# Pacing the weight loads of the last attention head, and five smaller reorderings, in a fused forward and backward pass

## The chip, the cores and the metric

The kernel runs on one core of one Trainium2 chip. The metric is device microseconds (us) of one execution on that core. A kernel is run several times, and its median is quoted.

## The reference

One attention block (32 heads of width 128 over 2048 positions, model width 576, cached K and V) times the silu of a gated feed-forward block (hidden width 4608), both on the layer norm of `x`, with a residual. The kernel returns the forward result and the gradients of eight arguments.

```python
def _fwd_reference(A_x, A_k_cache, A_v_cache, A_wq, A_wo, B_x, B_w_gate, B_w_up, B_w_down):
    ...
    x = A_x
    xn = _layernorm(x, axis=-1)
    s = _A_ref(xn, A_k_cache, A_v_cache, A_wq, A_wo)      # softmax attention, then @ wo
    g = _silu(_B_ref(xn, B_w_gate, B_w_up, B_w_down))     # (sigmoid(xn@wg) * (xn@wu)) @ wd
    return x + s * g

def reference(A_x, ..., grad_out):
    ...
    _out, _vjp = jax.vjp(_f, A_x, A_k_cache, A_v_cache, A_wq, A_wo, B_w_gate, B_w_up, B_w_down)
    return (_out, *_vjp(grad_out))
```

## The kernel before

The kernel begins with the layer norm and the feed-forward block's forward pass. Attention, forward and backward, one head after the other, is the long stage in the middle. Then comes the first late stage (the product with `wo`), the feed-forward's backward pass, the gradient of `wq`, and a last stage for the gradient of `x`.

**Attention.** A head has two phases of 16 slots each, one slot for 128 query rows. Phase 1 makes a slab of probabilities with `exp` on ScalarE, and SyncE transposes it by DMA. Phase 2 makes the backward slab from `dp` in two halves, and that slab is transposed by DMA too. What uses a transposed slab (`tail1`, `tail2`) comes five slots later (the skew).

```python
def transpose_slab(hs, qt, name):
    T = wpt.tile([P, NT, P], bf, name=name, tag="PT")
    nc.sync.dma_start_transpose(T[:], hs.slabs[qt][:])          # PT or dST, 512 KB
    return T
...
def main2(hs, qt, hf):                                          # phase 2, half hf of row block qt
    Pq, hsl = hs.slabs[qt], slice(hf * HW_, (hf + 1) * HW_)
    dp = ps_big.tile([P, HW_], f32, name="dp", tag="big")
    ... # 2 matmuls into dp
    if hf == NHF - 1:
        nc.vector.scalar_tensor_tensor(Pq[:, hsl], dp[:], hs.negdelta[:, qt:qt + 1], Pq[:, hsl], op0=ALU.add, op1=ALU.mult)
        hs.dST[qt] = transpose_slab(hs, qt, "dST")
    else:
        t = wt.tile([P, HW_], bf, name="t")
        nc.scalar.activation(t[:], dp[:], AF.Identity, bias=hs.negdelta[:, qt:qt + 1], scale=1.0)
        nc.vector.tensor_tensor(Pq[:, hsl], t[:], Pq[:, hsl], op=ALU.mult)
```

**Loads for the first late stage.** The stage after attention needs all of `wo` (4608 KB) and the attention outputs ("on rows") transposed. Both go into buffers that fall free during the last head. `wo` is loaded by GpSimd, four heads at a time.

```python
bl = 2 * NT * (H - 1) + NT                                      # slot where phase 2 of the last head begins
for view, h0, n, dead in wo_parts:
    for k in range(0, n, 4):
        at = (1 + k // 4, q(skew + 1), q(skew + 2), q(skew + 4), q(skew + 5))[dead]
        put(bl + q(at), 0, lambda view=view, h0=h0, k=k, n=n: load_wo_rows(view, h0, k, min(k + 4, n)))
for st in range(min(2, NT)):
    put(bl + NT + skew * st, 0, lambda st=st: load_oT(oTs[st], st))
```

**The layer norm** is interleaved with feed-forward matmuls. A `turn` is five TensorE transposes of a normed row block.

```python
def turn_step():
    if todo["turn"] and not (todo["norm"] and todo["norm"][0] <= todo["turn"][0]):
        st = todo["turn"].pop(0)
        turn(st)
```

**Further on**, `load_heads` loads the on rows and the `dq` rows of the first head group together. In the last stage ScalarE's and VectorE's row sums go into two halves of one small tile, `cc`.

Of the kernel before, what the change touches and what calls it, by code (L numbers as in the profile page):

```python
# [66 lines left out]
def kernel(  # L67
# [164 lines left out]
    with tc.tile_pool(name="pa", bufs=1) as pa:  # L232
# [75 lines left out]
        with tc.tile_pool(name="a1w", bufs=1) as wp:  # L308
# [37 lines left out]
            with tc.tile_pool(name="a0", bufs=3) as sb0, tc.tile_pool(name="a0ps", bufs=2, space=PSUM) as ps0, \  # L346
# [70 lines left out]
                def turn_step():  # L417
                    if todo["turn"] and not (todo["norm"] and todo["norm"][0] <= todo["turn"][0]):
                        st = todo["turn"].pop(0)
                        turn(st)  # L420
                        return st
# [168 lines left out]
    def attention(fast):  # L590
        with ExitStack() as es:
# [15 lines left out]
            acc_box[0] = acc_alloc  # L607

# [85 lines left out]
            def main2(hs, qt, hf):  # L694
                Pq, hsl = hs.slabs[qt], slice(hf * HW_, (hf + 1) * HW_)
                dp = ps_big.tile([P, HW_], f32, name="dp", tag="big")
                for c in range(HW_ // CH):
                    nc.tensor.matmul(dp[:, c * CH:(c + 1) * CH], lhsT=hs.dOT[:, qt * P:(qt + 1) * P],  # L698
                                     rhs=hs.VT[:, hf * HW_ + c * CH: hf * HW_ + (c + 1) * CH], start=True, stop=True)
                if hf == NHF - 1:  # L700
                    nc.vector.scalar_tensor_tensor(Pq[:, hsl], dp[:], hs.negdelta[:, qt:qt + 1], Pq[:, hsl], op0=ALU.add, op1=ALU.mult)  # L701
                    hs.dST[qt] = transpose_slab(hs, qt, "dST")
                else:
                    t = wt.tile([P, HW_], bf, name="t")
                    nc.scalar.activation(t[:], dp[:], AF.Identity, bias=hs.negdelta[:, qt:qt + 1], scale=1.0)  # L705
                    nc.vector.tensor_tensor(Pq[:, hsl], t[:], Pq[:, hsl], op=ALU.mult)  # L706

# [68 lines left out]
            def q(k):  # L776
                return min(k, NT - 1)
# [46 lines left out]
            for view, h0, n, dead in wo_parts:  # L824
                for k in range(0, n, 4):
                    at = (1 + k // 4, q(skew + 1), q(skew + 2), q(skew + 4), q(skew + 5))[dead]
                    put(bl + q(at), 0, lambda view=view, h0=h0, k=k, n=n: load_wo_rows(view, h0, k, min(k + 4, n)))
# [35 lines left out]
    with late("pc") as pc, late("pcw") as pcw, late("pcf") as pcf, \  # L863
# [123 lines left out]
        def load_heads(on_, dq_, hg):  # L987
            nc.gpsimd.dma_start(on_, rows_view(on2_d, hg * HG * P, HG * P))
            nc.gpsimd.dma_start(dq_, rows_view(dq2_d, hg * HG * P, HG * P))

        with late("b1r", 2) as dblk, late("b1l") as ldp, late("b1t", 3) as tmpp, late("b1o", 2) as outp, \
# [5 lines left out]
            for fb in range(NFB):  # L997
# [10 lines left out]
                dg_blk = dblk.tile([P, NT, FB], bf, name="dg_blk")  # L1008
                for st in range(NT):
# [13 lines left out]
                if fb == NFB - 1:  # L1023
                    nc.gpsimd.dma_start(ds_all, rows_view(ds_d, 0, D))
                    load_heads(onb0, dqb0, 0)
# [5 lines left out]
                for (blk_, out_, nm) in ((du_blk, out_7, "dwu"), (dg_blk, out_6, "dwg")):  # L1031
# [7 lines left out]
                    store_T(out_, fcols, stg_)  # L1039
        pc2.release()  # L1040
# [34 lines left out]
        with late("c2w") as wp, late("c2b") as blk, late("c2s", 2) as sb, late("c2ps", 4, space=PSUM) as ps:  # L1075
# [3 lines left out]
            for hg in range(NHG):  # L1079
                cols = slice(hg * HG * P, (hg + 1) * HG * P)  # L1080
                onb, dqb = onqs[hg % 2]
                if hg + 1 < NHG:
                    load_heads(*onqs[(hg + 1) % 2], hg + 1)
# [17 lines left out]
        with late("c4s", 2) as sb, late("c4cf") as chp, late("c4ps", 2, space=PSUM) as ps:  # L1101
# [10 lines left out]
            class Rows:  # L1112
# [24 lines left out]
                def finish(self):  # L1137
                    nj = len(ncs)
                    for sl in range(nsl):
# [3 lines left out]
                        cc = sb.tile([P, 2, nj], f32, name="cc")  # L1143
                        junk = sb.tile([P, D], f32, name="junk")
                        for j, (n0, nn) in enumerate(ncs):
                            nc.scalar.activation(dxn[:, n0:n0 + nn], self.accs[sl][j][:, :nn], AF.Copy, accum_out=cc[:, 0, j:j + 1])  # L1146
                            nc.vector.scalar_tensor_tensor(junk[:, n0:n0 + nn], self.accs[sl][j][:, :nn], 1.0, xn_all[:, st, n0:n0 + nn],  # L1147
                                                           op0=ALU.mult, op1=ALU.mult, accum_out=cc[:, 1, j:j + 1])
                        cs = sb.tile([P, 2], f32, name="cs")
                        nc.vector.tensor_reduce(cs[:], cc[:], axis=AX.X, op=ALU.add)  # L1150
# [54 lines left out]
```

## Time and profile before

| | before |
|---|---|
| median of 4 runs | 5043.6 us (5036.5 to 5046.4) |
| profiled execution | 5055.3 us, span 5053.4 us |
| TensorE busy | 4922.4 us |
| start to the end of the feed-forward's forward matmuls | 338.5 us |
| a middle head: phase 1 + phase 2 | 49.40 + 48.29 us |
| the last head: phase 1 + phase 2 | 72.15 + 63.34 us |

The profiled execution is 12 us slower than the median.

The stage lengths are read from the timeline of TensorE: from the first matmul of one stage to the first of the next. The windows view gives, for a stretch of time, its length, then the busy us and the number of instructions of TensorE, the weight loads, VectorE, ScalarE and GpSimd, then the granted clock, the mean share of the DMA engines and GB/s. Here are a middle head and the two phases of the last head of the kernel before:

```profile
2330.00:2428.00 98.00, 96.71 (x1251) 77.82 (x1269) 62.54 (x165) 67.03 (x113) 17.19 (x29) 1.00 1.02 209
3514.40:3586.50 72.10, 53.24 (x635) 42.49 (x644) 26.77 (x112) 37.29 (x69) 10.32 (x15) 0.86 1.16 194
3586.50:3650.00 63.50, 54.67 (x779) 46.50 (x787) 38.06 (x56) 27.61 (x43) 10.46 (x16) 1.00 1.08 210
```

In the middle head TensorE is busy for 96.7 of 98 us, and the DMA share is already above 1 (the records of transfers overlap). In phase 1 of the last head TensorE works for 53 of 72 us while the DMA engines are as full as ever and move less (194 GB/s). The costliest groups of the page that the change touches (line, engine, operation, tiles, count, then busy us, mean ns of one, and the idle time just ahead of them):

```profile
L705 ACT ACTIVATE t<-dp,negdelta 128x1024 bf16<-128x1024 f32 x512 | 571.1, 1116 | 222.6 <-PE dp L698 169.0
L698 PE MATMUL dp<-VT,dOT 128*128 128x512 bf16 x1728 | 540.0, 379 | 7.6 <-DVE Pq L701 7.6
```

The only wait of TensorE that the profile lists in a middle head's phase 2 is that of the second line: 7.6 us over all 32 heads.

### The profile page before, as it was taken

To read this page: it belongs to the slowest core of one execution; us is meant where nothing else is said; L and a number is where in the kernel's file an instruction comes from. 1 tells how busy PE (TensorE), PEld (TensorE's weight loads), DVE (VectorE), ACT (ScalarE), POOL (GpSimd) and SP (SyncE) were. 2 spreads that over 40 slices of the span, in tenths; PEclk is the share of its full clock that TensorE was granted. 3 is DMA by queue.
4 is the path that set the end of the run, shared out by engine and by line. 5 is a ranking of instruction groups with operands and counts; after the bars stand their busy time and mean duration, and the time that the engine had idled before them with its cause. 6 is when DMAs were issued, how large, how long until landed. Compare 5 with 4: busy or idle time off the path is not lost.

```text
span 5053.4 us, 128161 instructions
## 1 busy us (share of the span) xinstructions
PE 4922.4 (97%) x53584; PEld 3474.9 (69%) x54480; DVE 2581.2 (51%) x6705; ACT 2574.1 (51%) x4636; POOL 950.4 (19%) x1481
## 2 busy tenths in 40 slices
PE   8999999999999999999999999999789999999999
PEld 3445777777777787777778777777646666555554
DVE  4544666666566666666656666665425444200111
ACT  4432766666666676666667666666313333211000
POOL 3322111111111111111111111111122222211000
PEclk9999999999999999999999999999999999999999
DMA  7886999999999999999999999999996665797976
GB/s 249 271 202 171 212 208 211 203 211 209 207 214 214 201 212 207 210 205 211 214 202 209 215 206 207 208 213 202 197 201 204 193 183 181 213 266 187 173 141 121
DMA packets 2762675, 1031.39 MB, mean 204 GB/s; under 512 B 2665249, under 2 KB 2669474, under 8 KB 2762082
## 3 DMA queue, kind: packets, MB, share of 16 engines
q1 hardware_dynamic: 2659746, 699.38, 75.0%
q0 software_dynamic: 101728, 323.05, 20.1%
q8 instruction: 428, 7.01, 0.6%
q14 instruction: 165, 1.35, 0.1%
q10 hardware_dynamic: 608, 0.59, 0.0%
HBM read 175.31 MB, written 182.13 MB: 71 GB/s over the span
## 4 chain that ended last, share of the span: by engine, by line
PE 89%; issue 4%; DMA 3%; DVE 2%; ACT 1%; POOL 0%; SPq 0%; POOLq 0%; ACTq 0%; DVEq 0%
PE acc L734 17%; PE acc L675 17%; PE acc L960 13%; PE sp L628 7%; PE acc L1131 7%; PE dp L698 7%; PE acc L213 6%; PE g_ps L446 3%; PE u_ps L448 3%; PE dh L1013 3%; PE acc L531 2%; PE acct L146 2%; PE acc L930 2%; DMA dST<-Pq 1%; DVE Pq L701 1%
## 5 line engine op out<-in xcount | busy, mean ns | idle before, releaser
L646 ACT ACTIVATE Pq<-sp 128x1024 bf16<-128x1024 f32 x1024 | 1047.1, 1023 | 330.4 <-PE sp L628 199.1
L734 PEld LDWEIGHTS <-Pq 128*128 128x128 bf16 x16384 | 1002.9, 98 | 240.5 <-issue 1.1
L705 ACT ACTIVATE t<-dp,negdelta 128x1024 bf16<-128x1024 f32 x512 | 571.1, 1116 | 222.6 <-PE dp L698 169.0
L701 DVE SCALAR_TENSOR_TENSOR Pq<-dp,negdelta,Pq 128x1024 bf16<-128x1024 f32 x512 | 654.9, 1279 | 38.6 <-PE acc L675 37.5
L675 PEld LDWEIGHTS <-PT 128*128 128x128 bf16 x8192 | 503.3, 98 | 142.2 <-DMA PT<-Pq 20.9
L675 PE MATMUL acc<-Vn,PT 128*128 128x128 bf16 x8192 | 548.4, 219 | 26.6 <-DMA PT<-Pq 19.6
L675 PE MATMUL acc<-Kn,dST 128*128 128x128 bf16 x8192 | 551.3, 219 | 10.1 <-DMA dST<-Pq 6.5
L734 PE MATMUL acc<-dOn,Pq 128*128 128x128 bf16 x8192 | 547.4, 219 | 10.2 <-DVE junk L687 0.2
L628 PE MATMUL sp<-KQ 128*128 128x512 bf16 x1762 | 548.4, 380 | 2.6 <-ACT Pq L646 2.4
L698 PE MATMUL dp<-VT,dOT 128*128 128x512 bf16 x1728 | 540.0, 379 | 7.6 <-DVE Pq L701 7.6
L734 PE MATMUL acc<-Qn,Pq 128*128 128x128 bf16 x8192 | 540.6, 219 | 3.4
L706 DVE TENSOR_TENSOR Pq<-t,Pq 128x1024 bf16<-128x1024 bf16 x512 | 354.3, 692 | 365.8 <-ACT t L705 359.0
L675 PEld LDWEIGHTS <-dST 128*128 128x128 bf16 x8192 | 492.0, 98 | 69.5 <-DMA dST<-Pq 8.6
L715 ACT ACTIVATE dq_n<-acc,rsc 128x128 bf16<-128x128 f32 x512 | 188.1, 367 | 333.0 <-PE acc L675 331.9
L1147 DVE SCALAR_TENSOR_TENSOR junk<-acc,xn_all 128x512 f32<-128x512 f32 (+1 forms) x32 | 13.9, 453 | 637.0 <-ACT dxn L1146 637.0
L748 POOL DMA_DIRECT2D out_dram<-kvo x256 | 140.2, 548 | 1019.0 <-DVE kvo L746 1011.0
L669 POOL DMA_DIRECT2D on_d<-o_n x128 | 97.0, 758 | 750.7 <-DVE junk L687 396.7
L1015 DVE TENSOR_TENSOR du_blk<-dh,ah 128x256 bf16<-128x256 f32 x288 | 120.1, 417 | 191.6 <-PE dh L1013 189.5
L50 DVE TENSOR_SCALAR o_n<-acc,rinv_all 128x128 bf16<-128x128 f32 x352 | 123.2, 350 | 180.9 <-PE acc L675 180.9
L1146 ACT ACTIVATE dxn<-acc 128x512 f32<-128x512 f32 (+1 forms) x32 | 12.8, 406 | 393.6 <-PE acc L1131 386.2
L633 DVE TENSOR_REDUCE rs_all<-rsp 128x1 f32<-128x2 f32 x512 | 78.0, 152 | 256.3 <-ACT Pq L646 254.1
L646 ACT ACTIVATION_READ_ACCUMULATOR Pq<-sp 128x1 f32 x1024 | 200.4, 196 | 0.0
(206 smaller groups left out, 6949.9 us busy)
## 6 DMA issues: line engine op xcount, KB each, us to landing
out_dram<-kvo POOLq DMA_DIRECT2D x256, 128.0 KB, 4.2
ah<-a_d POOLq DMA_DIRECT2D x18, 1024.0 KB, 7.1
ah<-h_d POOLq DMA_DIRECT2D x18, 1024.0 KB, 9.5
du_d<-du_blk POOLq DMA_DIRECT2D x18, 1024.0 KB, 8.1
dg_d<-dg_blk POOLq DMA_DIRECT2D x18, 1024.0 KB, 9.9
h_d<-h_row POOLq DMA_DIRECT2D x64, 256.0 KB, 3.5
a_d<-a_row POOLq DMA_DIRECT2D x64, 256.0 KB, 3.7
x_all<-in_A_k_cache_dram SPq DMA_DIRECT2D x64, 256.0 KB, 4.0
```

The source lines that it names most:

```text
L213: nc.tensor.matmul(av[:, :CH], lhsT=w[:, i, :], rhs=srcT[:, i, cs], start=(i == 0), stop=(i == DT - 1))
L628: nc.tensor.matmul(sp[:, c * CH:(c + 1) * CH], lhsT=hs.QT[:, qt * P:(qt + 1) * P], rhs=hs.KT[:, hf * HW_ + c * CH: hf * HW_ + (c + 1) * CH ...
L646: nc.scalar.activation(Pq[:, hsl], sp[:], AF.Exp, scale=SCALE, accum_out=hs.rsp[:, hf:hf + 1])
L675: nc.tensor.matmul(hs.acc[:, 0, :], lhsT=T[:, kt, :], rhs=rhs[:, kt, :], start=(kt == 0), stop=(kt == NT - 1))
L698: nc.tensor.matmul(dp[:, c * CH:(c + 1) * CH], lhsT=hs.dOT[:, qt * P:(qt + 1) * P], rhs=hs.VT[:, hf * HW_ + c * CH: hf * HW_ + (c + 1) * C ...
L701: nc.vector.scalar_tensor_tensor(Pq[:, hsl], dp[:], hs.negdelta[:, qt:qt + 1], Pq[:, hsl], op0=ALU.add, op1=ALU.mult)
L705: nc.scalar.activation(t[:], dp[:], AF.Identity, bias=hs.negdelta[:, qt:qt + 1], scale=1.0)
L706: nc.vector.tensor_tensor(Pq[:, hsl], t[:], Pq[:, hsl], op=ALU.mult)
L715: nc.scalar.activation(hs.dq_n[:, qt % G4, :], hs.acc[:, 0, :], AF.Copy, scale=hs.rsc[:, qt:qt + 1])
L734: nc.tensor.matmul(self.tile[:, j, :], lhsT=self.slabs[qt][:, kt * P:(kt + 1) * P], rhs=self.rhs[:, qt, :], start=(qt == self.lo), stop=(q ...
L960: nc.tensor.matmul(accs[j][:, :nn], lhsT=lhs[:, st, cols], rhs=rhs[:, st, n0:n0 + nn], start=(st == 0), stop=(st == NT - 1))
L1131: nc.tensor.matmul(self.accs[sl][j][:, :nn], lhsT=ch[:, kk, sl * P:(sl + 1) * P], rhs=wT[:, k0 + kk, n0:n0 + nn], start=(self.k + kk == 0) ...
```

## The change

The intent is to spread the 4608 KB of `wo` over the last head so that they don't hold up the slab transposes, and to close five small waits. The parts keep the letters of the prediction.

- **A**: `wo` loads two heads at a time, in chosen slots from the start of phase 1 of the last head. A one-element GpSimd copy that reads the slab of the slot keeps each load from being hoisted ahead of that slot.
- **B**: in the layer norm, a transpose may not follow its own norm in the very next step.
- **C**: a dummy `exp` before attention, so that the table is loaded ahead.
- **D**: in the first row block of phase 2, VectorE takes the first half and ScalarE the second.
- **E**: the `dq` rows are loaded one step earlier, apart from the on rows.
- **F**: separate accumulator tiles for ScalarE and VectorE in the last stage.

```diff
-                    if todo["turn"] and not (todo["norm"] and todo["norm"][0] <= todo["turn"][0]):
+                    if todo["turn"] and not (todo["norm"] and todo["norm"][0] <= todo["turn"][0] + 1):
 ...
+            warm = stat.tile([P, 1], f32, name="warm")
+            nc.scalar.activation(warm[:], eps_t[:], AF.Exp)
 ...
-                if hf == NHF - 1:
+                if (hf == NHF - 1) != (qt == 0 and NHF > 1 and hf in (0, NHF - 1)):
                     nc.vector.scalar_tensor_tensor(Pq[:, hsl], dp[:], ...)
-                    hs.dST[qt] = transpose_slab(hs, qt, "dST")
                 else:
                     ...
+                if hf == NHF - 1:
+                    hs.dST[qt] = transpose_slab(hs, qt, "dST")
 ...
-            for view, h0, n, dead in wo_parts:
-                for k in range(0, n, 4):
-                    at = (1 + k // 4, q(skew + 1), q(skew + 2), q(skew + 4), q(skew + 5))[dead]
-                    put(bl + q(at), 0, lambda view=view, h0=h0, k=k, n=n: load_wo_rows(view, h0, k, min(k + 4, n)))
+            dead_from = (5 - NT, 5 - NT, skew + 2, NTH + 2, -NT)
+            free = [k for k in range(-NT, NT) if k < 3 - NT or (k > 3 - NT and k % 2)]
+            free += [k for k in range(skew + 2, NT) if k % 2 == 0]
+
+            def paced(slot, view, a, b):
+                hs = heads[H - 1]
+                nc.gpsimd.tensor_copy(view[0:1, a, 0:1], hs.slabs[slot % NT][0:1, 0:1])
+                load_wo_rows(view, view_h0[id(view)], a, b)
+            view_h0 = {}
+            for view, h0, n, dead in sorted(wo_parts, key=lambda w: dead_from[w[3]]):
+                view_h0[id(view)] = h0
+                for k in range(0, n, 2):
+                    at = min([f for f in free if f >= dead_from[dead]] or [NT - 1])
+                    if at in free:
+                        free.remove(at)
+                    put(bl + at, 0, lambda at=at, view=view, k=k, n=n: paced(at, view, k, min(k + 2, n)))
 ...
+                if fb == NFB - 1:
+                    ...
+                        load_dq(dqb0, 0)
 ...
-                    load_heads(onb0, dqb0, 0)
+                    load_on(onb0, 0)
 ...
-                        cc = sb.tile([P, 2, nj], f32, name="cc")
+                        ca = sb.tile([P, nj], f32, name="ca")
+                        cb = sb.tile([P, nj], f32, name="cb")
```

More of the change, by code (lines that the diff above doesn't have):

```diff
@@ L985, with load_on, load_dq @@
         assert HG * P <= 2 * FB
-        def load_heads(on_, dq_, hg):
+        def load_on(on_, hg):
             nc.gpsimd.dma_start(on_, rows_view(on2_d, hg * HG * P, HG * P))
+        def load_dq(dq_, hg):
             nc.gpsimd.dma_start(dq_, rows_view(dq2_d, hg * HG * P, HG * P))
@@ L1008 @@
                 dg_blk = dblk.tile([P, NT, FB], bf, name="dg_blk")
+                if fb == NFB - 1:
+                    if NFB % 2:
+                        dqb0_late = True
+                    else:
+                        dqb0_late = False
+                        load_dq(dqb0, 0)
                 for st in range(NT):
@@ L1039 @@
                     store_T(out_, fcols, stg_)
+            if dqb0_late:
+                load_dq(dqb0, 0)
         pc2.release()
@@ L1082 @@
                 if hg + 1 < NHG:
-                    load_heads(*onqs[(hg + 1) % 2], hg + 1)
+                    load_on(onqs[(hg + 1) % 2][0], hg + 1)
+                    load_dq(onqs[(hg + 1) % 2][1], hg + 1)
                 dwq = dwqs[hg % 2]
@@ L1142, in finish @@
                         dxn = sb.tile([P, D], f32, name="dxn")
-                        cc = sb.tile([P, 2, nj], f32, name="cc")
+                        ca = sb.tile([P, nj], f32, name="ca")
+                        cb = sb.tile([P, nj], f32, name="cb")
                         junk = sb.tile([P, D], f32, name="junk")
                         for j, (n0, nn) in enumerate(ncs):
-                            nc.scalar.activation(dxn[:, n0:n0 + nn], self.accs[sl][j][:, :nn], AF.Copy, accum_out=cc[:, 0, j:j + 1])
+                            nc.scalar.activation(dxn[:, n0:n0 + nn], self.accs[sl][j][:, :nn], AF.Copy, accum_out=ca[:, j:j + 1])
                             nc.vector.scalar_tensor_tensor(junk[:, n0:n0 + nn], self.accs[sl][j][:, :nn], 1.0, xn_all[:, st, n0:n0 + nn],
-                                                           op0=ALU.mult, op1=ALU.mult, accum_out=cc[:, 1, j:j + 1])
+                                                           op0=ALU.mult, op1=ALU.mult, accum_out=cb[:, j:j + 1])
                         cs = sb.tile([P, 2], f32, name="cs")
-                        nc.vector.tensor_reduce(cs[:], cc[:], axis=AX.X, op=ALU.add)
+                        nc.vector.tensor_reduce(cs[:, 1:2], cb[:], axis=AX.X, op=ALU.add)
+                        nc.vector.tensor_reduce(cs[:, 0:1], ca[:], axis=AX.X, op=ALU.add)
                         m12 = sb.tile([P, 2], f32, name="m12")
```

## The prediction

> **What bounds the kernel now.** I read the page first (busy shares, then the shares of the chain that ended last), then the list of waits for TensorE alone, then timelines where those waits lie.
>
> ```profile
> PE 4922.4 (97%) x53584; PEld 3474.9 (69%) x54480; DVE 2581.2 (51%) x6705; ACT 2574.1 (51%) x4636; POOL 950.4 (19%) x1481
> PE 89%; issue 4%; DMA 3%; DVE 2%; ACT 1%; POOL 0%; SPq 0%; POOLq 0%; ACTq 0%; DVEq 0%
> ```
>
> TensorE is busy for 4922.4 of 5053.4 us, and 89% of the chain is TensorE. No part of the change takes away a matmul, so all that can be won is in the 131 us (5053.4 - 4922.4) in which TensorE has nothing to do, plus the time in which it runs slowly after a pause. The waits of TensorE say where (columns: total us, times, longest us):
>
> ```profile
> PE acc L675 <- DMA PT<-Pq: 19.6, 3, 15.4
> PE pt L376 <- ACT x_all L370: 14.5, 9, 8.3
> PE dp L698 <- DVE Pq L701: 7.6, 32, 0.2
> PE acc L675 <- DMA dST<-Pq: 6.5, 9, 1.4
> PE acc L960 <- DMA ah<-dq_d: 2.9, 1, 2.9
> PE sp L628 <- ACT Pq L646: 2.4, 1, 2.4
> ```
>
> Each part of the change answers to one of these lines. Attention is the long stage (490 to 3650 us). Taking the first score matmul (sp) and the first dp matmul of each head from the timeline, phase 1 takes 49.40 us and phase 2 48.29 us, the same to 0.01 us in nearly all heads. Only the last head is different: its phase 1 goes from 3514.39 to 3586.54, 72.15 us, which is 22.75 us too long. The timelines of TensorE and GpSimd show why:
>
> ```profile
> 3541.70 0.59 PE L628 MATMUL sp<-KQ 128*128 128x512 bf16 x2
> 3557.66 1.89 PE L675 MATMUL acc<-Vn,PT 128*128 128x128 bf16 x16 [15.37 <-DMA PT<-Pq]
> ...
> 3529.13 1.50 POOL L573 DMA_DIRECT2D dsT<-in_A_wo_dram  x2 [4.88 <-PE acc L213]
> 3532.15 0.75 POOL L573 DMA_DIRECT2D dsT<-in_A_wo_dram  x1
> 3534.35 1.29 POOL L573 DMA_DIRECT2D dsT<-in_A_wo_dram  x2
> 3537.68 0.75 POOL L573 DMA_DIRECT2D Kn<-in_A_wo_dram  x1
> ```
>
> The wo rows are meant for phase 2 of the last head in program order, but the scheduler hoists them to when their buffers are dead: within 9 us it issues 4 x 576 + 144 + 432 = 2880 KB. TensorE then stands 15.37 us for a transposed probability slab. The DMA view shows the two queues in 27 us of that burst, and below in 27 us of a middle head (packets, MB, share of 16 engines; q1 carries the slab transposes, q0 the GpSimd loads and stores):
>
> ```profile
> q0 software_dynamic: 905, 3.42, 63.9%
> q1 hardware_dynamic: 3030, 0.76, 49.3%
> ...
> q1 hardware_dynamic: 16432, 4.15, 77.8%
> q0 software_dynamic: 224, 0.54, 5.9%
> ```
>
> The transposes get 0.76 MB instead of 4.15 MB through.
>
> **What the Trainium skill says.** (1) "DMA: Bandwidth & Descriptors", section SWDGE vs HWDGE vs iDMA: loads from GpSimd and transposes from SyncE feed different queues inside the same engine, which takes turns between them, switching at packet boundaries. The trace agrees in kind: a plain packet moved 3.42 MB / 905 = 3.8 KB, a transpose packet 0.25 KB, so equal turns give transposes little while plain packets wait. (2) "TensorE: Matmul & The Clock Gate", section What's actually happening: after a window of some 3.4 us idle the array runs at half clock until it has been busy as long. The trace agrees: after the pause 16 small matmuls took 1.89 us, against 1.06 usually. (3) "ScalarE: Activation LUTs", section What ACT_TABLE_LOAD costs: about 1.28 us for a load, plus a drain. The trace has the 1.28 us; it shows no drain.
>
> **The change part by part.**
>
> A, wo rows. Before: 10 loads of 144 to 576 KB. After: 18 of at most 288 KB (3 into xnT, 9 into dsT, 2 each into Kn, Vn, dOn), the same 32 x 144 = 4608 KB. Ahead of each a one-element copy on GpSimd reads the probability slab of its slot, so the load can't be hoisted ahead of that slot. The slots are the first three of phase 1, then every other one, with four more late in phase 2 as spares; the last load falls near slot 12 of phase 2. A slot is 49.40 / 16 = 3.1 us, so 288 KB every 6.2 us instead of 2880 KB in 9 us. The 18 copies lie beside everything: GpSimd is 19% busy. What can come back: 22.75 us in phase 1. In the rest of the head, from 3586.54 to the first matmul of the next stage at 3649.89, 63.35 us pass. Expected from other heads: 48.29, less the preparation of a next head that is not there (16 transposes 0.89, 5 transposes 0.28, 4 groups of 5 wide matmuls at 1.08 = 4.32: together 5.5), plus tails that else run in the next head (5 x 0.89 = 4.5, and 128 small matmuls at 0.0558 = 7.1): 54.4. So 9.0 us too many, of which 2.48 is a wait at the stage boundary that the change doesn't touch: 6.5 us. A's ceiling is 22.75 + 6.5 = 29.2 us. Not all comes back, as all bytes still share the engines. In the middle head the transposes ran at 4.15 / 27 = 0.154 MB/us, while single stretches of that view reach about 0.29 MB/us, so there is room to catch up between loads, and five slots of skew (15 us) against a median landing time of 4.9 us to absorb a delay. I leave 7 us as lost: **A = 22 us**.
>
> B, layer norm. A transpose may now follow the norm of its row block by one more step. In the first seven blocks the order doesn't change by the new rule. It changes for the last nine:
>
> ```profile
> 53.00 0.45 PE L376 MATMUL pt<-ident,x_all 128*128 128x128 bf16 x5 [3.50 <-ACT x_all L370]
> 60.24 0.45 PE L376 MATMUL pt<-ident,x_all 128*128 128x128 bf16 x5 [0.41 <-ACT x_all L370]
> 78.19 0.45 PE L376 MATMUL pt<-ident,x_all 128*128 128x128 bf16 x5 [0.36 <-ACT x_all L370]
> ```
>
> A step without a transpose takes 2.16 us here, and 5 transposes add 0.24, so nine steps are 21.6 us. They take from 49.5 to 78.19 + 2.41 = 80.6, 31.1 us: 9.5 us lost. After the change the first transpose still meets a norm that ends at 52.95, as the statistics, the table load and the root are ahead of it; TensorE gets there one step later (51.65), which leaves about 1.3 us, perhaps 0.3 on the next, and some slow clock. ScalarE needs 0.60 + 0.86 + 0.69 = 2.15 us a step, under TensorE's 2.40, so the later waits go. **B = 6.5 us**.
>
> C, exp table. The load stands between the first finished scores and the first exp:
>
> ```profile
> 492.65 1.28 ACT L646 ACT_TABLE_LOAD   x1 [1.71 <-PE acc L213]
> 495.11 0.59 PE L628 MATMUL sp<-KQ 128*128 128x512 bf16 x2 [2.45 <-ACT Pq L646]
> ```
>
> ScalarE idles 1.71 us just before, so the load fits there, and TensorE's wait of 2.45 loses 1.28. **C = 1.3 us**, once.
>
> D, first half of phase 2 on VectorE. TensorE waits 0.24 us in each of 32 heads (7.6 in the list) because VectorE takes the second half 0.85 us late (dp done 3467.56, op starts 3468.41). With halves swapped, ScalarE takes the second half at once (1.11 us), and VectorE the first (1.28 us). But VectorE also has row sums and the scaling of the last dOn block to do there, which TensorE needs 1.3 us later. The best case is 7.6, the worst a loss of several tenths a head: **D = 4 us**.
>
> E, dq load a step earlier. It now precedes the stores and two other loads, 2 MB that move while the engines are all but idle (65 GB/s mean in the 17 us before the stores). The wait of 2.87 goes, with some 1.3 us of slow clock after it; the load of on rows gets its end no sooner, so its wait of 0.84 may grow. **E = 3 us**.
>
> F, separate accumulator tiles at the end. VectorE starts 0.7 us sooner in the last block, but has two more reductions at 0.16 us. **F = 0.4 us**.
>
> Sum: 22 + 6.5 + 1.3 + 4 + 3 + 0.4 = 37.2 us. I keep about 3 us back for effects on later DMA order, as several waits in the stage after attention (14.2 us in sum) hang on landing times: 5043.2 - 34.2 = **5009 us**, ratio 0.993.
>
> **Rivals.** First, DMA stays the bound of the last head: the same 4608 KB pass, and in the burst plain data moved at only 3.42 / 27 = 0.127 MB/us. If that were the rate at which spread loads move too, they would fill 36 us of the 110 and starve transposes meanwhile; for it speaks that transposes alone need over half of each head. Then A is 10 us and the time 5021. Against it: other heads take in 1 MB of K and V and more with 1.29 us of TensorE idle. Second, D turns round: the scaling of dOn lands behind VectorE's 1.28 us op, and TensorE waits 0.5 to 0.9 us a head instead of 0.24, 8 to 20 us lost instead of 4 won: 5021 to 5033. For it: VectorE is late there already. Against: the scheduler can put other matmuls first. Third, everything works, with A and D at their ceilings: 29 + 7 + 1.3 + 7.6 + 4 + 0.4 = 49, time 4994.
>
> **Range and chances.** From the third rival and a bit below to between the first two: 4991 to 5027. 2% is 101 us, more than all that is idle where the change acts; there is no transfer or operation added that could cost 101 us. Faster by over 2%: 0.01, within 2%: 0.98, slower: 0.01.
>
> **What would show it right or wrong.** A: 18 wo loads some 6 us apart, phase 1 of the last head 50 to 56 us, no TensorE wait on PT above 3 us; a phase 1 of 60 us or more says the first rival. B: the total for x_all falls from 14.5 to about 10, of which 8.3 is the start. C: the table load ends before the first scores. D: the 32 waits of 0.2 us vanish and a middle head takes 97.4 instead of 97.69 us; a longer head says the second rival. E: no wait on dq, perhaps a longer one on the on rows. The prediction is wrong if the time is over 5027, most likely by D, which alone is multiplied by 32.

## The result, and the profile after

| | before | after |
|---|---|---|
| median | 5043.6 us (5036.5 to 5046.4, 4 runs) | 5019.6 us (5016.5 to 5026.4, 4 runs) |
| ratio, 95% interval | | 0.9956 (0.9939 to 0.9974) |
| a second set, in another session | 5045.2 us (11 runs) | 5016.4 us (6 runs), ratio 0.9940 (0.9924 to 0.9957) |
| span of the profiled execution | 5053.4 us | 5024.2 us |

The result is correct. The change gives 24 us in the first set and 29 us in the second. The profiled execution of after is, like that of before, a slow one: 5026.4 us, the slowest of its four.

Cut into stages, the two profiled executions compare as follows (us):

| stage | before | after | difference |
|---|---|---|---|
| layer norm and feed-forward forward | 338.49 | 331.07 | -7.42 |
| up to attention | 151.91 | 151.91 | 0.00 |
| head 0 | 90.02 | 90.91 | +0.89 |
| the 30 middle heads | 2933.98 | 2922.41 | -11.57 |
| last head, phase 1 | 72.15 | 52.19 | -19.96 |
| last head, phase 2 | 63.34 | 71.24 | +7.90 |
| first late stage (`wo`) | 145.54 | 148.04 | +2.50 |
| feed-forward backward, first part | 559.00 | 558.85 | -0.15 |
| from there to the last stage | 279.91 | 275.45 | -4.46 |
| last stage | 407.69 | 410.73 | +3.04 |
| tail | 11.07 | 11.07 | 0.00 |

The sum of the differences is -29.2 us, which is 5024.2 - 5053.4. Head 0 took between 89.4 and 91.5 us in the kernels, whatever its code (but for one told of below), so its +0.89 is put down to no part. The page of after, with the lines that answer to those shown of before:

```profile
PE 4914.6 (98%) x53584; PEld 3475.1 (69%) x54480; DVE 2582.2 (51%) x6721; ACT 2575.9 (51%) x4637; POOL 961.8 (19%) x1507
PE 92%; DMA 3%; issue 3%; DVE 1%; ACT 0%; SPq 0%; POOL 0%; POOLq 0%; ACTq 0%; DVEq 0%
L706 ACT ACTIVATE t<-dp,negdelta 128x1024 bf16<-128x1024 f32 x512 | 568.1, 1116 | 178.4 <-PE dp L700 123.0
L700 PE MATMUL dp<-VT,dOT 128*128 128x512 bf16 x1728 | 540.8, 379 | 0.0
```

TensorE has as many matmuls as before and is busy 7.8 us less; groups of 16 small matmuls that follow a long pause take 1.89 us instead of 1.07, and there are fewer such pauses; how much of the 7.8 us that makes wasn't summed. The chain that ended last is 92% TensorE in place of 89%. The idle time ahead of `dp` is gone: that is part D. TensorE's waits in after (total us, times, longest):

```profile
PE pt L376 <- ACT x_all L370: 10.5, 4, 8.5
PE acc L677 <- DMA PT<-Pq: 10.1, 2, 7.5
PE acc L945 <- DMA KQ<-on_d: 8.8, 2, 8.1
PE acc L677 <- DMA dST<-Pq: 5.5, 6, 1.6
PE acc L945 <- DMA xnT<-on_d: 4.6, 1, 4.6
PE acc L945 <- issue: 3.0, 3, 2.5
PE sp L630 <- ACT Pq L648: 2.1, 1, 2.1
```

The wait for `PT` has halved, from 19.6 to 10.1 us, and isn't gone. Those for `dp` and for the `dq` rows are gone. The windows view of a middle head and of the two phases of the last head, in after:

```profile
2326.50:2423.90 97.40, 96.34 (x1243) 77.57 (x1262) 62.22 (x164) 66.79 (x112) 17.16 (x28) 1.00 1.08 210
3496.30:3548.50 52.20, 49.05 (x636) 39.40 (x644) 27.04 (x112) 37.26 (x69) 13.40 (x26) 1.00 1.14 230
3548.50:3619.70 71.20, 57.34 (x777) 48.25 (x784) 38.03 (x56) 27.68 (x43) 16.44 (x32) 0.93 1.07 217
```

Phase 1 of the last head is nearly what a middle head's is, at 230 GB/s. Phase 2 has become the slow one: 71.2 us, with 13.9 us in which TensorE doesn't work. The timeline of TensorE in after shows the two waits for `PT`. The later one falls in the first slots of phase 2, where the last slabs of phase 1 are used:

```profile
3543.17 1.07 PE L677 MATMUL acc<-Vn,PT 128*128 128x128 bf16 x16 [2.62 <-DMA PT<-Pq]
...
3566.73 1.89 PE L677 MATMUL acc<-Vn,PT 128*128 128x128 bf16 x16 [7.46 <-DMA PT<-Pq]
```

The timeline of SyncE in after shows what stood ahead of those slabs in its queue (start, length of the issue, the transfers):

```profile
3531.00 4.97 SPq L582 DMA_TRANSPOSE xnT<-on_d  x1
3536.39 17.40 SPq L624 DMA_TRANSPOSE PT<-Pq  x6
3553.88 6.48 SPq L582 DMA_TRANSPOSE KQ<-on_d  x1
3560.45 4.25 SPq L624 DMA_TRANSPOSE PT<-Pq  x1
```

Each wait comes after a transpose of on rows (1 MB each, twice a slab). These transposes are in the program for the first late stage, later than the last head, and are hoisted to where their buffers fall free. The `wo` loads themselves are paced as intended. From the timeline of GpSimd in after:

```profile
3516.86 0.72 POOL L573 DMA_DIRECT2D dsT<-in_A_wo_dram  x1 [0.40 <-POOL dsT L833]
3522.88 0.71 POOL L573 DMA_DIRECT2D dsT<-in_A_wo_dram  x1 [0.38 <-POOL dsT L833]
3528.29 0.71 POOL L573 DMA_DIRECT2D dsT<-in_A_wo_dram  x1 [0.36 <-POOL dsT L833]
```

They come 5 to 8 us apart in most of phase 1. All 18 are out by 3593.5.

### The profile page after: what moved, and what is told of

The parts are those of the page before. It is cut to its first block, busy times and chain, and to the rows that moved or that the text cites. A ratio compares the mean times of both kernels' runs of the same rounds, so it can differ in the third digit from the quotient of the medians.

```text
span 5024.2 us, 128236 instructions
## 1 busy us (share of the span) xinstructions
PE 4914.6 (98%) x53584; PEld 3475.1 (69%) x54480; DVE 2582.2 (51%) x6721; ACT 2575.9 (51%) x4637; POOL 961.8 (19%) x1507
## 4 chain that ended last, share of the span: by engine, by line
PE 92%; DMA 3%; issue 3%; DVE 1%; ACT 0%; SPq 0%; POOL 0%; POOLq 0%; ACTq 0%; DVEq 0%
PE acc L737 18%; PE acc L677 18%; PE acc L975 13%; PE sp L630 8%; PE dp L700 7%; PE acc L1157 6%; PE acc L213 6%; PE u_ps L448 3%; PE g_ps L446 3%; PE dh L1036 3%; PE acc L531 3%; PE acct L146 2%; PE acc L945 2%; DMA dST<-Pq 1%; DMA xnT<-on_d 1%
## 5 line engine op out<-in xcount | busy, mean ns | idle before, releaser
L677 PE MATMUL acc<-Vn,PT 128*128 128x128 bf16 x8192 | 547.4, 219 | 17.0 <-DMA PT<-Pq 10.1
L737 PE MATMUL acc<-dOn,Pq 128*128 128x128 bf16 x8192 | 552.3, 219 | 10.1
L1174 DVE SCALAR_TENSOR_TENSOR junk<-acc,xn_all 128x512 f32<-128x512 f32 (+1 forms) x32 | 13.9, 453 | 635.6 <-ACT dxn L1173 635.6
```

The costliest lines, as they stand in the source:

```text
L677: nc.tensor.matmul(hs.acc[:, 0, :], lhsT=T[:, kt, :], rhs=rhs[:, kt, :], start=(kt == 0), stop=(kt == NT - 1))
L737: nc.tensor.matmul(self.tile[:, j, :], lhsT=self.slabs[qt][:, kt * P:(kt + 1) * P], rhs=self.rhs[:, qt, :], start=(qt == self.lo), stop=(q ...
```

## The experiments

All kernels below gave correct results, and each verdict against before was "same" at 2%, except that of `warm_pers`. The theory of the prediction was that the `wo` burst starves the slab transposes, so that pacing removes the wait. Its main rival was that the last head simply has more DMA work than its time allows, so that waits move within the head. (In the expectations below, theory 1, T1 and T2 are names that each text gives to theories of its own: in `ot_late` and `skip_slots` T1 is the transposes of on rows, T2 the `wo` loads alone.) Four groups of runs follow.

### 1. Which part gives how much: a_only, no_a, d_only, bcef (one chip, before 5048.3 us)

`a_only` is the kernel before with part A alone.

```diff
# before, plus only
-            for view, h0, n, dead in wo_parts: ... (loads of four heads)
+            dead_from = ...; free = ...; def paced(...) ... (loads of two heads, paced)
```

> Kernel before plus the wo loads of the changed kernel alone (two heads at a time, each behind its one-element copy). Theory 1, the parts act in separate stages and add up: phase 1 of the last head takes about 52 us (72.15 before, 52.19 after), and from the start of its phase 2 to the next stage about 71 us (63.35 before, 71.24 after), other heads stay at 49.40 and 48.29, layer norm and later stages as before; in sum 12 us less, about 5031. Rival: the longer phase 2 of the last head comes from another part of the change, which shifted things there; then it takes about 63 us here and the time is about 5023.

Measured: 5042.7 us, ratio 0.9983 (0.9956 to 1.0009). The last head took 56.12 + 74.54 = 130.7 us.

`no_a` is the kernel after with the old `wo` loads.

```diff
# after, with
-            dead_from = ... (paced loads)
+            for view, h0, n, dead in wo_parts: ... (the loads of before)
```

> Changed kernel with the wo loads of the kernel before. Theory 1, the parts add up: first scores near 483, middle heads 49.40 and 47.97 us, phase 1 of the last head about 72 us, from there to the next stage about 63; about 22 us less than before (7.4 + 0.3 + 10.2 + 4.5), 5021, so nearly the time of the changed kernel although its largest term is missing. Rival: the wo loads are worth the 20 us by which they shorten phase 1, and the time is about 5040.

Measured: 5019.8 us, ratio 0.9939 (0.9910 to 0.9969). The last head took 59.79 + 70.51 = 130.3 us.

`d_only` is before with the swapped halves.

```diff
# before, plus only
-                if hf == NHF - 1:
+                if (hf == NHF - 1) != (qt == 0 and NHF > 1 and hf in (0, NHF - 1)):
```

> Kernel before with only the swapped halves at the start of phase 2. Theory: phase 2 of a middle head 47.97 us in place of 48.29, no wait of dp for VectorE at L701, 10 us less over 32 heads, about 5033. Rival: the 0.32 us a head in the changed kernel came from another schedule that the other parts caused; then 48.29 stays and the time is 5043.

Measured: 5036.6 us, ratio 0.9971 (0.9943 to 0.9999). The 30 middle heads took 2923.45 us against 2933.98.

`bcef` is before with B, C, E and F.

```diff
# before, plus
+ turn_step: "+ 1";  warm exp;  load_on / load_dq apart;  ca and cb in place of cc
```

> Kernel before with the layer norm order, the exp table, the early dq load and the split accumulators, without the wo loads and the swap. Theory: first scores at about 483 (490.4 before), first phase of head 0 0.3 us shorter, the stage from the last dh to the last stage 4.5 us shorter (279.9 before, 275.4 after); heads as before; about 12 us less, 5031. If the last stage is 3 us longer here as in the changed kernel, that loss belongs to these parts; if it is as before (407.7 us), it belongs to the wo loads or the swap, or to chance.

Measured: 5036.5 us, ratio 0.9969 (0.9938 to 0.9999).

What follows: D gives 11.8 us by the medians and B, C, E, F together give 11.8 too. Their ratios multiply to 0.9971 x 0.9969 = 0.9940, and `no_a`, which has exactly these, measured 0.9939. So within the intervals (some 15 us wide on either side) these parts add up, and together they are as large as the whole change. `a_only` is 5.6 us below before by the medians, but its interval holds 1, and its last head, with the paced loads, is no shorter than that of `no_a`. In this comparison nothing clear of noise is left for A. And `no_a` also shows why: with the old loads its last head took 130.3 us, not the 135.5 us of the profiled execution of before, and `d_only` (128.4) and `bcef` (129.6) agree. The profile that the prediction read was a slow draw just there.

### 2. Pacing, splitting, and where the wait goes: split_nopace, skip_slots, ot_late (one chip, before 5043.6 us)

`split_nopace` keeps the loads of two heads each and takes away the copy that ties a load to its slot.

```diff
             def paced(slot, view, a, b):
                 hs = heads[H - 1]
-                nc.gpsimd.tensor_copy(view[0:1, a, 0:1], hs.slabs[slot % NT][0:1, 0:1])
                 load_wo_rows(view, view_h0[id(view)], a, b)
```

> Changed kernel with the 18 loads of two heads but without the one-element copies, so that the scheduler may hoist them. If the pacing is what matters: the loads into dsT go out in one burst, phase 1 of the last head 58 to 72 us as in the four executions with the old loads, time like the kernel without the new loads, 5020. If the smaller size of a load matters by itself: phase 1 of 52 to 56 us as with the paced loads.

Measured: 5023.8 us, ratio 0.9966 (0.9935 to 0.9997), last head 60.69 + 64.13 = 124.8 us. The timeline of GpSimd:

```profile
3505.08 1.42 POOL L573 DMA_DIRECT2D dsT<-in_A_wo_dram  x2 [0.92 <-PE acc L213]
3509.04 2.11 POOL L573 DMA_DIRECT2D dsT<-in_A_wo_dram  x3 [2.54 <-PE acc L213]
3512.09 1.41 POOL L573 DMA_DIRECT2D dsT<-in_A_wo_dram  x2
3514.26 1.27 POOL L573 DMA_DIRECT2D dsT<-in_A_wo_dram  x2
```

The nine loads into `dsT` come within 10 us again, and phase 1 is back at 60.7 us. Splitting does nothing for phase 1 by itself. It is the false dependence on the slab that spreads the loads and shortens phase 1. The last head as a whole, at 124.8 us, is only 1.4 us longer than in after.

`skip_slots` keeps the pacing and leaves out the slots around the change of phase, where the waits of after lie.

```diff
-            free += [k for k in range(skew + 2, NT) if k % 2 == 0]
+            free = [k for k in free if k < -1 or k > 3] + [k for k in range(4, NT) if k % 2 == 0]
```

> Changed kernel with no wo loads in slots -1 to 3 around the start of phase 2; they come later in phase 2, more closely. T2 (wo loads alone starve the transposes): no PT wait of 7 us at the start of phase 2, that part falls from 71 to about 64, though the waits for dST later may grow by some us. T1 (the on-row transposes in SyncE's queue): the wait at the start of phase 2 stays, 70 us or more. Time 5012 under T2, 5020 under T1.

Measured: 5027.0 us, ratio 0.9967 (0.9938 to 0.9997), last head 53.80 + 80.70 = 134.5 us. TensorE's waits:

```profile
PE acc L677 <- DMA dST<-Pq: 14.4, 9, 6.1
...
PE acc L677 <- DMA PT<-Pq: 5.9, 2, 3.3
```

With no `wo` load near it, the wait for `PT` at 3563.9 fell from 7.46 to 3.35 us. That suggests that the loads had a share in it; the rest stayed. The loads pushed to later slots then held up the transposes of phase 2: `dST` rose from 5.5 to 14.4 us, and the head became 11 us longer. Neither theory of the expectation foresaw that: the wait halved where one said that it would go and the other that it would stay.

`ot_late` leaves the `wo` loads as they are in after and takes away the other suspect: the two transposes of on rows are tied to the last slab of phase 1, so that they can't go ahead of the slabs.

```diff
+                def late_oT(st):
+                    nc.gpsimd.tensor_copy(oTs[st][0:1, 0, 0:1], heads[H - 1].slabs[NT - 1][0:1, 0:1])
+                    load_oT(oTs[st], st)
-                put(bl + NT + skew * st, 0, lambda st=st: load_oT(oTs[st], st))
+                put(bl + NT + skew * st, 0, lambda st=st: late_oT(st))
```

> Changed kernel, but the first two transposes of on rows for the next stage (1 MB each, on SyncE's queue with the slab transposes) are held back to the end of the last head by a one-element copy that reads the last slab. Theory T1: in the changed kernel these two sit in the queue ahead of slab transposes just before the two TensorE waits of 2.62 and 7.46 us for PT; without them both waits go, phase 1 of the last head takes at most 51 us and from phase 2 to the next stage about 61 us in place of 71.24; the next stage may wait up to 3 us more for its rows; some 10 us less than the changed kernel, about 5010. Rival T2: the wo loads alone starve the slab transposes; then the PT waits stay near 10 us and the time near 5020.

Measured: 5010.8 us, ratio 0.9941 (0.9910 to 0.9972), last head 49.40 + 72.93 = 122.3 us. TensorE's waits:

```profile
PE acc L677 <- DMA dST<-Pq: 9.7, 12, 2.7
PE acc L948 <- DMA out_dram<-kvo: 5.7, 1, 5.7
...
PE acc L677 <- DMA PT<-Pq: 1.1, 2, 0.9
```

The wait for `PT` is gone and phase 1 takes exactly what a middle head's takes, 49.40 us. So the transposes of on rows, and not the `wo` loads alone, were what stood ahead of the late `PT` slabs. But the last head as a whole is hardly shorter than in after (122.3 against 123.4): `dST` and the stage boundary wait for what `PT` no longer waits for. That is what the prediction's first rival said ("DMA stays the bound of the last head"). Of this run's own expectation, the waits for `PT` and the time (about 5010) came true, but phase 2 took 72.93 us where about 61 was expected. The time was met by luck: against the profiled execution of after, the last head gave 1.1 us and the first late stage 14.3 (133.7 against 148.0 us), and group 3 shows that the latter varies as much between executions of one kernel.

### 3. The direct comparison: after_b, no_a_b, no_a_ot, best (one chip, 6 runs each, before 5045.2 us)

The first group gave A nothing clear, but compared `no_a` with after across sessions. Here the same kernels run side by side. `after_b` is the kernel after, unchanged; `no_a_b` is `no_a` again.

> The changed kernel again, to be compared on one chip with the other three. By the stage marks of single executions so far, the time from the start of phase 1 of the last head to the next stage was 135.5, 130.3, 128.4, 129.6 us with the old wo loads (the kernel before was the slowest draw) and 123.4, 130.7 with the paced ones. If paced loads are worth anything they are worth about 4 us: 5020, some 4 less than the kernel without them. As predicted on record they would be worth 22.

Measured: 5016.4 us (5011.9 to 5023.1), ratio 0.9940 (0.9924 to 0.9957). Last head 53.69 + 68.83 = 122.5 us, first late stage 133.7 us.

> Changed kernel with the wo loads of the kernel before, again, on one chip with the changed kernel. 0 to 8 us slower than it if the paced loads only move the waits of the last head from phase 1 to phase 2; 20 us slower if the prediction on record had the size right.

Measured: 5028.7 us (5021.5 to 5032.9), ratio 0.9962 (0.9945 to 0.9978). Last head 61.53 + 63.78 = 125.3 us, first late stage 145.1 us.

`no_a_ot` is `no_a` with the on rows held back as in `ot_late`, so with the old loads.

```diff
# no_a, plus
+                def late_oT(st): ... (as in ot_late)
```

> Changed kernel with the wo loads of the kernel before, and the first two on-row transposes held back to the end of the last head. If these transposes alone made the waits: phase 1 of the last head near 50 us, time like the changed kernel with them held back, 5010. If the burst of wo loads does harm by itself: phase 1 58 us or more and about 5018. I lean to the second, as the burst went out just before the long PT wait.

Measured: 5014.9 us (5006.8 to 5021.0), ratio 0.9935 (0.9918 to 0.9952). Last head 56.87 + 67.06 = 123.9 us. Phase 1 lies between the two expectations (near 50, and 58 or more).

`best` is `ot_late` with another place for the dummy `exp` (group 4 tells why).

```diff
# ot_late, with
-            warm = stat.tile([P, 1], f32, name="warm")          # inside attention
+    warm = pers.tile([P, 128], f32, name="warm")               # ahead of the branch into attention
+    nc.scalar.activation(warm[:, 0:1], eps_t[:], AF.Exp)
```

> Changed kernel with the on-row transposes held back, and the warming exp ahead of the branch in a tile padded to 512 bytes a partition. The unpadded tile of 32 bytes moved all probability slabs and their transposes from addresses that are multiples of 512 to 32 above; if that is what cost 240 us, heads take 49.40 and 47.97 us again, and if not, 50.9 and 53.0 as there. With the table load ahead, phase 1 of head 0 is 40.1 us in place of 41.4. Phase 1 of the last head 49.4, time about 5008, 10 to 12 below the changed kernel.

Measured: 5011.5 us (5007.8 to 5019.3), ratio 0.9926 (0.9910 to 0.9941). Last head 49.40 + 72.99 = 122.4 us. That is 4.9 us below `after_b`, not 10 to 12, and phase 1 of head 0 took 43.3 us, not 40.1; the heads are as expected.

What follows: side by side, A is worth 12.4 us by the medians (11 by the means), more than the 0 to 8 us expected and less than the 20 of the prediction. The six runs of each hardly overlap (5011.9 to 5023.1 and 5021.5 to 5032.9 us), so on this chip A did gain. Over both sessions, with each kernel's ratios weighted by its runs, after is at (4 x 0.9956 + 6 x 0.9940) / 10 = 0.9946 and `no_a` at (4 x 0.9939 + 6 x 0.9962) / 10 = 0.9953. That is 3.5 us, with intervals of some 8 us or more on each. A is worth between nothing and 12 us, and these runs can't say where. In the profiled executions of this group the last head accounts for 2.8 us of the difference between `after_b` and `no_a_b`. Another 11.4 us is the first late stage, whose length differs from one execution to another without any change: after and `after_b` are the same kernel, and it took 148.0 us in one and 133.7 us in the other. TensorE's wait for `KQ<-on_d` there was 8.8 us in the first and 1.3 us in the second, and the 4.6 us for `xnT<-on_d` are missing in the second, so most of the spread follows when the first on rows land.

Holding back the on rows gives as much with the old loads (`no_a_ot`, 13.8 us less than `no_a_b`) as pacing the loads does (`after_b`), and both together (`best`) give 17.2 us, not the sum. The stages, one execution of each kernel, say how. Pacing takes 7.8 us off phase 1 of the last head with the on rows early (61.53 to 53.69) and 7.5 with them held back (56.87 to 49.40), so the burst does delay slabs by itself. But it gives 5.1 and 5.9 us back in phase 2, and the head gains only 2.8 and 1.5. The two parts compete for the same thing. `best` has the lowest median of the group. Its interval overlaps those of `after_b` and `no_a_ot`, so no winner is claimed.

### 4. Loading the exp table ahead of the branch: warm_pers (same chip as group 2)

In after the dummy `exp` stands at the start of attention, behind ScalarE's waits there. `warm_pers` moves it ahead of the branch, into a small tile of a pool that lives through the whole kernel.

```diff
-            warm = stat.tile([P, 1], f32, name="warm")
-            nc.scalar.activation(warm[:], eps_t[:], AF.Exp)
 ...
+    warm = pers.tile([P, 1], f32, name="warm")
+    nc.scalar.activation(warm[:], eps_t[:], AF.Exp)
```

> Changed kernel with the warming exp moved ahead of the branch, into a tile of memory that no earlier stage used. In the changed kernel ScalarE waits 1.29 us before the table load, until 484.81, at the place where it waited before; my theory is that its first tile in attention lies on memory of the stage before, whose last store had to land first. Then the load comes ahead of the wait, the first exp starts at about 484.8 in place of 486.21, phase 1 of head 0 is 1.3 us shorter (41.4 to 40.1). Rival: the first exp waits for something else as late; then it stays at 41.4. The time can't show 1.3 us.

Measured: 5258.3 us, ratio 1.0433 (1.0398 to 1.0467): slower. The heads take 50.9 + 53.0 us in place of 49.40 + 47.97. The waits of TensorE, and ScalarE's timeline:

```profile
PE acc L675 <- DMA dST<-Pq: 110.1, 73, 5.3
PE acc L675 <- DMA PT<-Pq: 83.7, 73, 8.3
```

```profile
1.79 1.28 ACT L859 ACT_TABLE_LOAD   x1 [1.79 <-issue]
3.09 0.20 ACT L859 ACTIVATE warm<-eps_t 128x1 f32<-128x1 f32 x1
3.31 1.28 ACT L362 ACT_TABLE_LOAD   x1
...
485.20 1.28 ACT L646 ACT_TABLE_LOAD   x1 [1.71 <-PE acc L213]
```

Two things happened, neither expected. First, the dummy `exp` (L859), which has nothing to wait for but `eps_t`, ran at 3.09 us, at the start of the kernel and not just ahead of the branch. Other functions' tables were loaded after it, at 3.31, 17.61, 49.23 and 53.12 us, so the first real `exp` needed a load again, at 485.20. The idea was never tested; the same holds for `best` (dummy at 3.08 us, load at 485.15). Second, the slab transposes became slower. From the view of the tile `PT`, its transposes' time to landing, first in after, then in `warm_pers`:

```profile
DMA to landing us min/median/max: 3.6/5.1/10.5
```

```profile
DMA to landing us min/median/max: 4.3/6.2/14.3
```

What differs for the slabs is their address, which is read from the built programs and not from a trace: the new tile takes 32 bytes of each partition, so the first probability slab moved from byte 16896 (33 x 512) to 16928, and the first `PT` from 90624 (177 x 512) to 90656. Other tiles moved along; those of K, Q and V did not. `best` tests this: it has the same dummy `exp` in the same pool, in a tile of 512 bytes. There the slabs and `PT` begin at multiples of 512 again (17408 and 91136), the median landing is 5.2 us and the heads take 49.40 + 47.97. `best` also holds back the on rows, but `ot_late`, which has only that, has the same heads, so this can't be what mends them. No run moved the slabs alone. The Trainium skill's page "DMA: Bandwidth & Descriptors", section How a descriptor splits into AXI transactions, says that a transaction must start at a multiple of 256 bytes and that a descriptor that doesn't start there costs extra beats. The runs agree in kind (32 bytes off, landings 1.1 us later, 22%); they don't show the beats themselves.

## Why the prediction was right or wrong

The prediction was 5009 us (4991 to 5027). The medians are 5019.6 and 5016.4 us, inside the range, 7 to 11 us above its middle. The direction and the class were right. The sum was less well founded than it looks: its largest term was too large, and two small ones were too small.

| part | predicted | measured | from |
|---|---|---|---|
| A | 22 | 0 to 12 | totals of group 1 and group 3 |
| B | 6.5 | 7.4 | first stage, 338.49 to 331.07 us |
| C | 1.3 | 0.3 | the wait of the second `sp`, 2.45 to 2.12 us |
| D | 4 | 10.2 | 32 x (48.29 - 47.97) us |
| E | 3 | 4.5 | stage 279.91 to 275.45 us |
| F | 0.4 | 0.0 | tail, 11.07 us in both |
| last stage | not foreseen | -2.5 | see below |

**A: the step that failed is its ceiling, "22.75 + 6.5 = 29.2 us".** It took one execution's excess over a middle head as the kernel's typical loss. Four other profiled kernels with the same loads had phases 1 of 58.8 to 62.6 us there, so of the 22.75 us only 9.4 to 13.2 were typical. The mechanism held in phase 1: in before the wait of 15.37 us ended at 3557.66, ahead of the first transpose of on rows (3567.88), so the burst made it without them; pacing brought phase 1 to 52.19 us, within the 50 to 56 foreseen, and `split_nopace` shows that pacing is the cause.

But the waits for `PT` were 9.6 to 14.7 us in those four kernels and still 10.1 and 7.9 in after and `after_b`. The second step that failed is that phase 2 would give back 6.5 us; it grew, by 7.9 us (the four kernels took 63.8 to 70.7 us there, so some of this is a draw too). The first rival named the likely reason, that "DMA stays the bound of the last head", and its numbers (A 10 us, time 5021) are nearer than the central ones, though its own sign, a phase 1 of 60 us or more, didn't show. The condition for the theory, no wait for `PT` above 3 us, was missed (7.46 us).

What neither had named is the transposes of on rows, which share SyncE's queue with the slabs. The windows of the last head show how much there is to move: in after the two data queues carry 19.75 + 7.47 = 27.2 MB in 123.4 us, 0.22 MB/us. A middle head carries 16.78 + 3.44 = 20.2 MB in 97.4 us, 0.21 MB/us, with TensorE fully busy. Of the difference, 3 MB are the three transposes of on rows that run in the last head, and most of the rest is `wo`. At a middle head's rate the last head's bytes would take 27.2 / 0.208 = 131 us. This is an estimate from those rows, and a rough one: after did it in 123.4 us, so the middle head's rate, where TensorE is the busy one, is no ceiling. What speaks for the queue is that after, `after_b`, `ot_late`, `no_a_ot` and `best` have last heads of 122.3 to 123.9 us, whichever wait is long in them, and that no kernel is below 122.3. But others are longer, `a_only` (130.7) with the same paced loads. That the DMA work is the bound there is therefore suggested and not shown; no run took bytes away from that head. The prediction's 54.4 us for phase 2 counted TensorE's work there and no transfers; no kernel took less than 63.3.

**B: right.** The first wait fell to 1.34 us (foreseen: about 1.3), the later ones went, and the total for `x_all` is 10.5 us (foreseen: about 10). The timeline of TensorE in after:

```profile
53.20 0.45 PE L376 MATMUL pt<-ident,x_all 128*128 128x128 bf16 x5 [1.34 <-ACT x_all L370]
...
55.86 0.45 PE L376 MATMUL pt<-ident,x_all 128*128 128x128 bf16 x5
...
58.31 0.44 PE L376 MATMUL pt<-ident,x_all 128*128 128x128 bf16 x5
```

The steps now follow at 2.44 us, and `bcef` repeats the stage at 330.97 us. The 0.9 us above the prediction fit the slow matmuls that it had left standing behind the first wait: in before five of them took 2.34 us there (at 54.55), in after 1.24 (at 54.57).

**C: wrong in its premise that the load fits into ScalarE's idle 1.71 us.** That idle time is a wait of ScalarE itself on entering attention, and the dummy `exp` stands behind it too. The timeline of ScalarE in after:

```profile
484.81 1.28 ACT L609 ACT_TABLE_LOAD   x1 [1.29 <-PE acc L213]
486.11 0.20 ACT L609 ACTIVATE warm<-eps_t 128x1 f32<-128x1 f32 x1
486.21 1.01 ACT L648 ACTIVATE Pq<-sp 128x1024 bf16<-128x1024 f32 x1
```

The first scores run from 482.98 to 483.57, so the table still loads after them. What ScalarE waits for there isn't settled. `warm_pers` and `best` were meant to test it and couldn't, since their dummy `exp` ran at 3 us and other tables came between (group 4).

**D: right in its sign and mechanism, mis-sized.** The 32 waits of 0.24 us vanished, and the second rival (the scaling of `dOn` landing late) didn't occur: `dp` waits for nothing. The term was put at half of its best case, 4 of 7.6 us. It measured 0.32 us a head, 10.2 us, and `d_only` confirms it alone (middle heads 10.5 us shorter). That it exceeds the wait of 0.24 us by 0.08 a head is measured, and its cause isn't shown.

**E: right, mis-sized by half.** No wait for `dq` is left, and the wait for the on rows didn't grow (0.76 us against 0.84). The stage is 4.5 us shorter in after and 4.1 in `bcef`, against 1.5 and 0.1 in `a_only` and `d_only`, which lack E.

**F: wrong.** VectorE still starts behind ScalarE in the last block, with separate tiles. The timeline of both engines in after:

```profile
5011.40 0.60 ACT L1173 ACTIVATE dxn<-acc 128x512 f32<-128x512 f32 x1 [48.11 <-PE acc L1157]
...
5012.12 0.69 DVE L1174 SCALAR_TENSOR_TENSOR junk<-acc,xn_all 128x512 f32<-128x512 f32 x1 [44.18 <-ACT dxn L1173]
```

The shared tile wasn't what tied them, and the 0.7 us are still there. What ties them wasn't tested.

**The last stage** took 410.7 to 413.7 us in the eight kernels that have extra one-element copies on GpSimd in the last head, and 407.7 to 409.3 us in the six that don't. This is an association in one execution of each; no run isolates it. It takes some 2.5 us off A's account.

Together, B, C, D, E and F measured 7.4 + 0.3 + 10.2 + 4.5 + 0 = 22.4 us against 15.2 predicted. That makes up for a good part of what A lacked, so that the time came out near the middle of the range is in part luck: errors of opposite sign.

## What to carry to other kernels

Before a wait in one profiled execution is taken as the price of something, look at the same place in other executions: here a slow draw doubled it. When a queue has more to move in a stage than the stage's time allows, spreading its transfers moves the waits from one tile to the next and may hardly shorten the stage, as here, so count its bytes, over all queues that feed the same engines, against the rate of an undisturbed stage; that is a rough guide (131 us by this count, 122 to 124 measured). A wait of 0.24 us that occurs once in each of 32 heads was worth as much as the burst that filled the waits list, and is much more surely had.

## What the Trainium skill lacked or had wrong

- **"DMA: Bandwidth & Descriptors", section DMA Transpose (X-bar).** Its table of constraints asks for 32-byte alignment in SBUF. A slab moved by 32 bytes keeps to that and is correct, but its transposes' median landing rose from 5.1 to 6.2 us and the kernel took 215 us longer than before; with the tile padded to 512 bytes, both went back (5.2 us). The page's section on AXI transactions gives the likely reason, the 256-byte boundary, but doesn't connect it with transposes or with where a pool places its tiles.
- **The same page, section SWDGE vs HWDGE vs iDMA.** It says that the queues share the engines, and gives no size for what plain loads do to transposes. In before 27 us with a burst of loads let 0.76 MB of transposes through, where 27 us of a middle head let 4.15 MB, and the three slab transposes issued in the burst took 26.6 us (median) to land, against 4.6.
- **"ScalarE: Activation LUTs", section What ACT_TABLE_LOAD costs.** The 1.28 us are confirmed. Of the drain of about 1.38 us no run shows anything after a load: in after the next ACTIVATE begins at 486.11, 0.02 us past the end of the table load that begins at 484.81. The 1.29 us ahead of that load are put down to a wait in the trace, and the loads at 17.65 and 53.16 us follow the operation before them without a pause.
